# A fused attention and ReGLU kernel whose order of operations comes from a table instead of a greedy planner

## The chip, the cores and the metric

The kernel runs on one core of one Trainium2 chip. The metric is the device time of one execution in microseconds; the median of three runs stands for it. The core has a matrix engine (TensorE, in profiles PE, with its weight loads as PEld), a vector engine (VectorE, DVE), an activation engine (ScalarE, ACT), a general engine (GpSimd, POOL) and an engine that only issues transfers here (SyncE, SP). Each engine runs its own instructions in the order of the program, and waits for the others through semaphores.

## What is computed

Causal attention with a window of 64 positions over 8 batches, 8 heads, 576 positions and 64 dimensions per head, and then a gated layer on all 4608 tokens:

```python
scores = scale * np.matmul(q, k.transpose(0, 1, 3, 2))
mask = (rel >= 0) & (rel < window)                 # window = 64
attn = softmax(np.where(mask, scores, -1e9))
x = np.matmul(attn, v)                             # -> [4608, 512]
gate = np.maximum(x @ w_gate, 0.0)                 # [4608, 1536]
val = x @ w_val
out = (gate * val) @ w_out                         # [4608, 512]
```

Inputs and output are float32; the kernel multiplies in float16 and accumulates in float32.

## The kernel before

**Tiles.** The tokens are cut into nine tiles of 512, numbered 0 to 8. `first_part` (L405 to L510) loads the first q, k, v and weights and computes most of tile 0's attention in an order written out by hand. `second_part` (L512 to L1090) makes the rest.

**Attention of a tile.** A `scores` operation (L385, with the mask added by L377) writes q times k of eight windows and four heads to four PSUM banks; four `exp` on ACT (L645) bring them to SBUF as p. Five `values` operations (L391) multiply by v. DVE takes the reciprocal of the row sums (`recip`, L660), multiplies (`norm`, L398) and transposes to x (`turn`, L403). The next batches' q and k come by `qk_load` on POOL (L347) and are transposed by `qk_turn` on DVE (L353); v comes by `v_load` on POOL (L356), and its shifted rows by `v_copy` (L608, L612, L616) or, from batch 2 on, by `v_move` on SP (L620).

**The gated layer of a tile.** Tile 0 uses plain products: `direct` (L750, a block of gate or value columns), then `relu0` (ACT, L760) and `mul0` (DVE, L762). Tiles 1 to 8 use Strassen-like products P1 to P7 of quarter matrices (L842): the weights' sums are made by `w_form` (L791), those of x by `x_form` (L716). Running sums are taken out of PSUM by `snap` on ACT (L851), completed by `sum` on DVE (L858); the gate half goes through `relu` on ACT (L867) or `last` (L889, straight out of PSUM), and `mult` on POOL (L876) gives the gated g. For one column group the chain between matmuls is short: P1, snap, P6, snap, P7, snap, P4, each product adding to the bank that the snap has just copied.

**The output.** Tiles 0 to 2 use plain `out` products (L916) with `evac` on ACT (L927) and `store` on SP (L931). Tiles 3 to 8 use seven products again (oP1 to oP7, L1005) with sums of g by `g_sum` on DVE (L973), sums of w_out by `wo_form` (L950), snaps (L1016), `osum` on DVE (L1041) and `evac` (L1044).

**What sets the order.** Every operation is an `Op` with a key (the time at which it is wanted, from the constants K), the engines that may run it with an assumed duration for each, the operations that it comes after, and the buffers that it takes and gives back: eight PSUM banks, ten p, twelve float32 `pr` buffers. `Plan.run` (L212 to L255) plays an event-driven schedule while the program is built: whenever an engine is free, `pick` (L178) takes the ready operation with the least key for which buffers are free, with a few rules (a POOL load is held back while the load queue is more than `bl` = 9 us long; a block of small matmuls waits when its instructions would come late). What `run` decides is only the order in which instructions are emitted and which buffer each takes. On the chip nothing of the planner is left: each engine has a fixed line of instructions. `fetch` (L103) is the planner's idea of when TensorE's instructions arrive, 256 at a time; `emit` adds an order between POOL and DVE operations that share a port (L1075 to L1086).

Of the operations, only `w_form`, `wo_form`, a few `x_form` and the `v_copy` may go to one of several engines; the greedy planner takes whichever is free first.

Of the kernel before, what the change touches and what calls it, by code (L numbers as in the profile page):

```python
# [10 lines left out]
FP32 = mybir.dt.float32  # L11
# [9 lines left out]
K = {"T1": 33.417, "STEP": 29.94, "wo1": 24.303, "wo2": 136.509, "q0": 0.81, "q1": 2.61, "q10": -9.561, "q11": 1.093, "v": -0.6, "v1": 1.142, "ql": 1.41, "qt": 0.88, "qti": 4.69, "vl": 0.91, "vc": 0.04, "vm": 1.83, "e": 7.62, "gap": 3.77, "gap1": -1.003, "r": -6.21, "tn": 1.66, "xf": 4.78, "wf": -1.338, "wfj": 2.6, "sn": 2.67, "su": -2.15, "re": 17.5, "mu": -6.61, "la": -4.79, "o0": 11.594, "o0j": 20.432, "o0s": -4.369, "oo": 0.007, "os": 0.386, "oj": 4.81, "gs": -1.18, "fo": 0.015, "fi": 0.098, "fs": 4.74, "fu": 0.27, "W0": 129.92, "TF": 3, "rs": 7.037, "rv": 3.751, "rt": 4.292, "wl": 1.63, "wln": 5.389, "l0": 0.003, "l1": 4.021, "lv": 1.186, "lvs": 12.368, "wo0": 25.921, "db": -7.955, "di": 1.563, "dv": 0.646, "slack": 0.3, "d2": 3.05, "bl": 9.0, "lv0": 18.364, "d": {'0:q0': 0.808, '0:fs': 1.88, '0:la': 1.692, '1:oo': 0.058, '0:fi': 0.024, '1:qt': 3.036, '1:os': -0.226, '0:vc': -1.15, '0:tn': -0.981, '0:qt': 0.904, '0:e': -2.629, '0:sn': 0.475, '0:vm': 0.58, '0:vl': 0.514, '0:ql': 0.128, '0:fu': -2.028, '1:tn': 3.174, '0:re': 0.858, '1:ql': -1.577, '0:xf': -0.14, '0:su': 0.053, '0:gap': 0.391, '0:r': -2.955, '0:oo': -0.042, '0:os': 0.025, '1:vm': 0.483, '1:fo': -0.017, '0:q1': 0.357, '1:sn': 0.632, '0:oj': -0.104, '0:qti': -0.947, '0:gs': -0.096, '0:fo': -0.029, '2:xf': -3.116, '1:oj': -0.851, '1:fu': -1.619, '1:gs': -1.956, '1:vl': 3.671, '1:fs': -1.692, '1:q0': -0.44, '1:re': 17.838, '1:qti': -0.251, '2:vl': -1.63, '1:xf': 0.54, '2:v': 0.897, '2:e': 3.091, '1:vc': -0.626, '2:gap': 1.519, '1:mu': -1.202, '2:oj': 1.272, '2:os': -0.152, '1:gap': -2.068, '1:su': 1.664, '1:q1': 0.09, '1:la': -0.927, '2:fu': -0.861, '2:q0': -1.678, '2:su': -3.121, '1:v': 0.703, '1:r': 0.099, '2:tn': 0.263, '2:mu': -0.767, '2:qti': -1.435, '2:sn': 0.235, '2:qt': 0.357, '3:re': -0.971, '3:su': 1.85, '2:gs': 0.316, '2:vc': -0.222, '2:fi': 0.018, '3:fs': 2.376, '2:oo': -0.024, '3:gs': -0.499, '2:ql': 2.087, '2:re': 1.781, '2:vm': -0.346, '2:la': -0.408, '3:fo': 0.105, '3:qt': -1.251, '3:qti': -0.756, '3:fi': 0.003, '3:r': 4.605, '4:tn': 4.441, '4:fo': 0.176, '3:sn': 1.86, '3:v': -0.191, '3:gap': 0.067, '3:q1': -1.861, '4:v': -2.381, '3:fu': -1.0, '3:e': -2.398, '3:ql': 0.244, '3:q0': -0.417, '4:ql': 1.859, '4:qti': -0.846, '3:oo': 0.017, '3:oj': -1.455, '3:mu': 5.549, '3:vl': -0.094, '3:la': -1.756, '3:os': 0.07, '4:qt': -2.162, '5:v': 2.345, '5:e': -6.12, '5:gap': -0.396, '4:re': 16.126, '4:r': -3.179, '4:os': 0.054, '4:q0': -0.903, '4:gap': -1.023, '4:fu': -1.144, '5:vm': 1.185, '4:fi': -0.029, '4:vm': 1.023, '4:la': 2.23, '4:vl': 0.037, '5:tn': -1.009, '5:r': -1.653, '5:fu': 0.073, '5:re': 3.794, '4:q1': 1.992, '4:sn': 1.164, '4:xf': -1.831, '5:fi': -0.019, '4:mu': 1.169, '4:oj': 1.089, '5:qti': -1.537, '5:fo': -0.021, '5:xf': -1.396, '5:gs': -0.82, '5:mu': -2.334, '5:vc': -0.566, '5:oo': 0.002, '5:q0': -0.047, '4:vc': 0.378, '5:qt': -1.506, '4:fs': 0.072, '5:ql': -0.361, '5:oj': 0.91, '5:fs': -0.532, '5:q1': -0.028, '4:oo': -0.002, '5:la': 0.275, '6:oo': -0.051, '6:vl': -1.345, '6:v': 0.087, '7:vc': 2.102, '6:os': 0.034, '7:fo': -0.026, '6:tn': -1.475, '6:gap': -1.442, '6:xf': 3.27, '6:fi': -0.035, '6:fo': -0.054, '6:fu': -0.179, '6:qt': 0.741, '7:tn': -0.289, '7:vl': -0.177, '6:ql': -0.604, '7:re': 9.431, '7:fi': 0.019, '7:xf': -0.992, '6:vc': -0.932, '7:sn': -0.018, '6:e': 6.905, '6:q1': 1.236, '7:ql': -0.482, '7:e': -4.862, '7:qt': 1.66, '6:mu': -0.73, '7:gap': 0.823, '6:oj': 0.303, '6:q0': 0.231, '6:r': 2.887, '7:su': 1.478, '7:gs': -0.403, '7:q0': -0.079, '7:q1': -0.303, '7:vm': -1.095, '6:gs': -0.02, '7:mu': -0.49, '7:fs': 1.309, '7:la': -0.048, '7:os': 0.117, '7:qti': -1.407, '7:r': -0.97, '7:fu': -0.866, '6:re': 0.021, '6:la': 0.896, '7:oo': -0.007, '6:sn': 0.915}}  # L21
# [5 lines left out]
class Op:  # L27


    def __init__(self, name, key, engines, fn, after, take, give, dma):  # L30
        self.small = 0
        self.count = 0
        self.opens, self.closes = None, False
# [6 lines left out]
        self.end = None  # L40
        self.on = None


class Plan:


    LAG = {"PE": 0.055, "ACT": 0.035, "DVE": 0.035, "POOL": 0.075, "SP": 0.06}
    DRAIN = 0.2
    AHEAD = 20.0
    TURN = 0.093  # L50
    LIMIT = 1e9
    FLIGHT = 8
    STAY = 4.0
# [3 lines left out]
    def __init__(self, free, queue, pools):  # L57
# [4 lines left out]
        self.taken = {}  # L62
        self.open = []
        self.filled = []
        self.known = {e: [] for e in free}
        self.waiting = {e: [] for e in free}
        self.times = []
# [20 lines left out]
    def know(self, o):  # L88
        for e in o.engines:
            self.known[e].append(o)  # L90
            heapq.heappush(self.times, o.ready[e])

    def fetch(self, n, t, dur, keep):
        at, asked, got, come = self.at, self.asked, self.got, list(self.come)
        end = at + n
        while True:
            ask, need = 256 * asked + self.ASK, 256 * got + self.NEED
            nxt = min(ask, need, end)
            t += (nxt - at) * dur / n
            at = nxt  # L100
            if at == end:
                break
            if ask <= need:  # L103
                begin = max([t] + come[-1:])
                begin += max(0.4, min(6.5, self.queue["q"] - begin), min(2.0, self.queue["sp"] - begin))
                come.append(begin + 2.4 + K["slack"])
                asked += 1
            else:
                t = max(t, come[got])
                got += 1  # L110
        if keep:
            self.at, self.asked, self.got, self.come = at, asked, got, come
        return t

    def fill(self, o, t, emit):
        if t - self.free["PE"] < 0.7:
            return
        free = [(self.taken[id(h[n])], h[n]) for pool, h, names in o.take if "bank" in pool for n in names]
        free += [(x[0], x[2]) for pool in ("bank", "bo") for x in self.pools[pool]]
        if free or self.open:  # L120
            since, bank = min(free, key=lambda x: x[0]) if free else (0.0, self.open[-1]["b"])
            since = max(self.free["PE"], since + 0.1)
            n = int((t - 0.25 - since) / 0.165)
            if n > 0:
                self.fetch(2 * n, since, 0.165 * n, True)
                self.filled.append((since, n, t, o.name))
                emit((bank, bool(free)), n)

    def finish(self, o, e, t, dur):
        if e == "PE":  # L130
            if o.opens is not None and o.opens in self.open:
                self.open.remove(o.opens)
            if o.opens is not None and not o.closes:
                self.open.append(o.opens)
            dur += self.TURN * ((o.small > 0) != self.small)
            self.small = o.small > 0
            if o.count:
                dur = self.fetch(2 * o.count, t, dur, True) - t
        end = t + dur
        self.free[e] = end  # L140
        heapq.heappush(self.times, end)
        o.on = e
        if o.dma:
            nbytes, rate, which = o.dma
            self.queue[which] = max(self.queue[which], end + 1.2) + nbytes / rate
            end = self.queue[which] + 0.8
            if e == "POOL":
                self.flight = self.flight[1:] + [end]
                heapq.heappush(self.times, self.flight[0] + 0.1)
# [14 lines left out]
    def grab(self, o, e, t):  # L164
        lag = self.LAG[e]
# [958 lines left out]
```

## Time and profile before

| | |
|---|---|
| median of three runs | 308.23 us (308.16 to 309.68) |
| span of the profiled execution, first to last instruction | 307.2 us |
| the median less that span | 1.0 us |
| TensorE granted clock | 0.999 |
| first matmul / last matmul's start | 1.3 / 303.1 us |
| matmuls | 4772 |
| snaps L851 on ACT | 144, 590 ns each |
| sums L858 on DVE | 144, 678 ns each |
| relus L867 on ACT | 72, 639 ns each |
| mults L876 on POOL | 96, 1283 ns each |
| x_forms L716 on POOL / DVE | 24 of 1160 ns / 8 |

The time of the profiled execution itself is not given apart from its span; the work is compared with the span, and the 1.0 us around it is added to come to the scale of the median. Busy time says how long an engine had an instruction at work. Matmuls are pipelined and the profile models their ends, so TensorE's holes are read from the starts: the distance between two starts, less the usual distance for that shape. An engine's row in a list of groups gives the count, the busy time, the mean duration, and after the bar the idle time just before these instructions with what ended it.

### The profile page before, as it was taken

The numbers are of one execution on the slowest core, as the hardware profiler recorded it, in microseconds if no ns is written. First come the engines' busy times: TensorE is split into PE (matmuls) and PEld (weight loads), VectorE is DVE, ScalarE is ACT, GpSimd is POOL, SyncE is SP. The second block draws the span as 40 slices with busy tenths as digits, with TensorE's granted clock in tenths as the row PEclk, the third lists the DMA queues.
The fourth block names the chain that finished last, engine by engine and source line by source line (L and its number), as shares of the span: only waits on it lengthen the run. The fifth ranks groups of instructions, "written<-read, shape, count | busy, mean of one in ns | idle before, by whom it ended". The sixth has DMA issues, their size and how long they took to land.

```text
span 307.2 us, 11254 instructions
## 1 busy us (share of the span) xinstructions
PE 297.1 (97%) x4772; PEld 240.2 (78%) x4772; DVE 246.2 (80%) x422; ACT 213.0 (69%) x414; POOL 229.8 (75%) x233
## 2 busy tenths in 40 slices
PE   7889999998999999999999999999999999999995
PEld 5475845786757886777888888888888888888884
DVE  5858997988963997887989988878896789595762
ACT  4445335897768787788778786778687886878721
POOL 8696957998999899999189954995479157938520
PEclk9999999999999999999999999999999999999999
DMA  7999999983249953996694194674112011201033
GB/s 219 187 190 206 196 194 198 202 169 22 19 78 150 183 99 75 139 182 136 123 72 82 34 165 120 48 166 37 54 36 69 6 38 37 68 0 36 1 121 120
DMA packets 59074, 32.87 MB, mean 107 GB/s; under 512 B 39440, under 2 KB 53392, under 8 KB 59024
## 3 DMA queue, kind: packets, MB, share of 16 engines
q0 software_dynamic: 46672, 18.29, 51.1%
q1 hardware_dynamic: 12208, 13.80, 14.2%
q8 instruction: 37, 0.61, 0.8%
q14 instruction: 13, 0.11, 0.1%
q10 hardware_dynamic: 144, 0.07, 0.1%
HBM read 37.75 MB, written 9.44 MB: 154 GB/s over the span
## 4 chain that ended last, share of the span: by engine, by line
PE 85%; DMA 8%; POOL 3%; issue 2%; DVE 1%; ACT 0%; ACTq 0%; DVEq 0%; POOLq 0%
PE bank L842 48%; PE bank L1005 18%; PE bank L916 8%; PE bank L391 4%; PE bank L750 3%; DMA wo<-in_moe_w_out_dram 3%; DMA wv<-in_moe_w_val_dram 3%; DMA k<-in_k_dram 2%; PE bank L385 2%; PE bank L377 1%; POOL vs L791 1%; POOL v L356 1%; POOL q L347 0%; POOL k L347 0%; DVE xw L398 0%
## 5 line engine op out<-in xcount | busy, mean ns | idle before, releaser
L876 POOL TENSOR_TENSOR g_sb<-pr,pr 128x512 f16<-128x512 f32 x96 | 121.6, 1283 | 47.7 <-ACT pr L889 16.5
L858 DVE TENSOR_TENSOR pr<-bank,pr 128x512 f32<-128x512 f32 x144 | 92.6, 678 | 24.7 <-PE bank L842 21.9
L851 ACT COPY pr<-bank 128x512 f32<-128x512 f32 x144 | 79.9, 590 | 30.2 <-PE bank L842 27.9
L842 PE MATMUL bank<-xt,vs 128*128 128x256 f16 x384 | 56.7, 273 | 0.0
L842 PE MATMUL bank<-xt,us 128*128 128x256 f16 x384 | 56.2, 273 | 0.0
L867 ACT ACTIVATE pr<-pr 128x512 f32<-128x512 f32 x72 | 45.4, 639 | 5.9 <-DVE pr L858 5.5
L842 PE MATMUL bank<-xt,wg 128*128 128x256 f16 x288 | 42.8, 273 | 0.0
L842 PE MATMUL bank<-xt,wv 128*128 128x256 f16 x288 | 42.7, 273 | 0.0
L842 PEld LDWEIGHTS <-us 128*128 128x128 f16 x384 | 37.0, 98 | 6.5 <-issue 0.2
L842 PEld LDWEIGHTS <-vs 128*128 128x128 f16 x384 | 37.2, 98 | 4.7
L645 ACT ACTIVATE p<-bank 128x512 f16<-128x512 f32 (+1 forms) x68 | 35.7, 592 | 6.7 <-PE bank L385 6.5
L916 PE MATMUL bank<-wo,g_sb 128*128 128x512 f16 x144 | 35.9, 380 | 0.3 <-DMA wo<-in_moe_w_out_dram 0.3
L356 POOL DMA_DIRECT2D v<-in_v_dram x40 | 34.9, 883 | 0.5 <-issue 0.5
L889 ACT ACTIVATE pr<-bank 128x512 f32<-128x512 f32 x48 | 27.1, 601 | 6.7 <-PE bank L842 5.0
L842 PEld LDWEIGHTS <-wg 128*128 128x128 f16 x288 | 27.7, 98 | 4.7
L842 PEld LDWEIGHTS <-wv 128*128 128x128 f16 x288 | 28.1, 98 | 4.2
L1005 PEld LDWEIGHTS <-g_sb 128*128 128x128 f16 x288 | 27.9, 98 | 3.4
L1005 PE MATMUL bank<-wo,g_sb 128*128 128x256 f16 x216 | 28.4, 273 | 0.0
L398 DVE TENSOR_TENSOR xw<-bank,r 128x448 f16<-128x448 f32 (+2 forms) x45 | 25.8, 575 | 1.5
L403 DVE STREAM_TRANSPOSE xt<-xw 128x512 f16<-128x512 f16 (+2 forms) x38 | 25.0, 668 | 0.5 <-ACT xw L506 0.3
L1005 PEld LDWEIGHTS <-ss 128*128 128x128 f16 x216 | 21.0, 98 | 2.5
L916 PEld LDWEIGHTS <-g_sb 128*128 128x128 f16 x144 | 13.5, 98 | 11.3 <-issue 0.3
(95 smaller groups left out, 389.4 us busy)
## 6 DMA issues: line engine op xcount, KB each, us to landing
out_dram<-pr SPq DMA_DIRECT2D x35, 256.0 KB, 2.4
k<-in_k_dram POOLq DMA_DIRECT2D x15, 288.0 KB, 7.5
q<-in_q_dram POOLq DMA_DIRECT2D x15, 288.0 KB, 7.1
v<-in_v_dram POOLq DMA_DIRECT2D x32, 128.0 KB, 6.4
v<-v SPq DMA_DIRECT2D x12, 132.0 KB, 2.6
v<-v SPq DMA_DIRECT2D x24, 66.0 KB, 2.3
wg<-in_moe_w_gate_dram POOLq DMA_DIRECT2D x6, 256.0 KB, 6.6
wv<-in_moe_w_val_dram POOLq DMA_DIRECT2D x6, 256.0 KB, 7.9
```

The costliest lines, as they stand in the source:

```text
L356: nc.gpsimd.dma_start(v16s[b % 2][lo:hi, g, :, 0:64], v[b, :, 64 * g - 64 + lo:64 * g - 64 + hi].rearrange("h p d -> p h d"))
L398: nc.vector.tensor_tensor(x, blocks_of(to, n)[:, :, 0:D].rearrange("p s (c e) -> p s e c", e=2), r[:, :, :, None].to_broadcast([128, n, 2, ...
L403: nc.vector.transpose(xt[:, 2 * hh:2 * hh + 2, c0:c0 + n].rearrange("p e (s c) -> p s e c", c=32), x)
L645: nc.scalar.activation(pp[g][:, 0:n].rearrange("p n c -> p (n c)"), st[g][:, 0:64 * n], ACT.Exp, scale=scale)
L842: nc.tensor.matmul(slot[to][:, HT * m:HT * m + HT], w[:, kk, 128 * m:128 * m + 128], x[:, kk], start=(first and m == 0 and kk == 0), stop= ...
L851: lambda e, hold=hold, slot=slot: nc.scalar.copy(hold["x"], slot["A"]),
L858: nc.vector.tensor_tensor(hold["x"], slot[to], hold["x"], ADD)
L867: lambda e: nc.scalar.activation(hold["x"], hold["x"], ACT.Relu), after=[o])
L876: lambda e: VEC[e].tensor_tensor(gh[:, fs:fs + 2, h], pair(a["x"]), pair(b["x"]), MUL),
L889: lambda e, hold=hold, slot=slot, i=i: nc.scalar.activation(hold["x"], slot["A"], ACT.Copy if i else ACT.Relu),
L916: nc.tensor.matmul(bank["b"][:, 0:c1 - c0], gs[t % 2][:, f, 128 * sub:128 * sub + 128], wo[:, f, c0:c1], start=(j == 0 and i == 0), stop=( ...
L1005: nc.tensor.matmul(bank[to][:, HD * m:HD * m + HD], a[:, f, 128 * m:128 * m + 128], b[:, f], start=(first and m == 0 and f == 0), stop=(f ...
```

## The change

The greedy choice is replaced by a table. `PLACES` holds 1609 numbers, one for each operation in the sequence in which `second_part` makes them; `ON` holds 487 digits, one for each operation that has more than one engine to choose from. `place` writes the place over the key and keeps only the chosen engine; `run` then takes each engine's operations strictly by place. The clock inside the planner still settles which of the engines goes next (and so which buffer is taken) but never the order within one.

```diff
+PLACES = [int(n) for n in """
+11 9 16 18 24 25 43 46 76 78 124 21 20 28 33 67 17 30 6 3 4 51 52 57 54 50 73 70 77 1 5 14 0 19 2 10 7 12 29 44 23 45 8 37 15 49 61 63 89 87
...
+ON = "".join("""
+20201100000010000001101010101001101101100100000102120110000000100000000000000000000000000000000000000001001100010000100111011000000000000000
...
+    def place(self, places, on):
+        choices = [o for o in self.all if len(o.engines) > 1]
+        assert len(places) == len(self.all) and len(on) == len(choices)
+        for o, n in zip(choices, on):
+            e = list(o.engines)[int(n)]
+            o.engines, o.ready = {e: o.engines[e]}, {e: o.ready[e]}
+        for o, key in zip(self.all, places):
+            o.key = key
...
     def run(self, emit):
+        lines = {e: sorted((o for o in self.all if e in o.engines), key=lambda o: (-o.key, -o.n)) for e in self.ENGINES}
+        for _ in self.all:
+            best = None
+            for e in self.ENGINES:
+                if lines[e] and not lines[e][-1].left:
+                    t = self.begin(lines[e][-1], e)
+                    if t is not None and (best is None or t < best[0] - 1e-12):
+                        best = t, e
...
+            t, e = best
+            o = lines[e].pop()
+            self.finish(o, e, t)
+            emit(o, e)
```

More operations get a choice, and small helpers give the instruction for either engine:

```diff
+    def copy_on(e):
+        return nc.scalar.copy if e == "ACT" else VEC[e].tensor_copy
+
+    def relu_on(e, to, x):
+        if e == "ACT":
+            return nc.scalar.activation(to, x, ACT.Relu)
+        else:
+            return VEC[e].tensor_scalar_max(to, x, 0.0)
...
-                forms.append(op("x_form", key + kt("xf") * gap + n, {**pool(512), **(dve16(512) if n == 1 or t == 1 else {})},
+                forms.append(op("x_form", key + kt("xf") * gap + n, any16(512),
...
-                        ran["snap", j, name, i] = op("snap", key - kt("sn"), act(512),
-                                                     lambda e, hold=hold, slot=slot: nc.scalar.copy(hold["x"], slot["A"]),
+                        ran["snap", j, name, i] = op("snap", key - kt("sn"), copies(512),
+                                                     lambda e, hold=hold, slot=slot: copy_on(e)(hold["x"], slot["A"]),
...
-                            ran["relu", j, n, h] = op("relu", key + kt("re"), {"ACT": (0.645, False)},
-                                                      lambda e: nc.scalar.activation(hold["x"], hold["x"], ACT.Relu), after=[o])
+                            ran["relu", j, n, h] = op("relu", key + kt("re"), {"ACT": (0.635, False), "DVE": (0.42, True)},
+                                                      lambda e: relu_on(e, hold["x"], hold["x"]), after=[o])
...
-                        o = op("mult", key + kt("mu"), pool(512),
+                        o = op("mult", key + kt("mu"), {**pool(512), "DVE": (0.68, True)},
```

`relu0`, `last`, the `evac` of the outputs, the output's snaps and `v_copy` get a choice in the same way. Read by the table, these operations run on another engine than before:

| operation | from | to | number |
|---|---|---|---|
| snap (12), last (5), evac (2), relu0 (3) | ACT | DVE | 22 |
| relu | ACT | DVE | 8 (tiles 2, 6, 7, 8) |
| mult | POOL | DVE | 6 (tiles 2, 6, 7 and three in 8) |
| x_form | POOL | DVE | 5, and 2 the other way |
| w_form, wo_form | DVE | POOL | 6, and 1 the other way |
| v_copy | DVE, POOL | ACT, POOL, DVE | 5 |

The rest of the diff changes the planner's own numbers: the times at which engines, banks and p buffers come free at its start, the assumed speed of the load queue, the model of the instruction fetch, a few durations. They reach the chip only through the order of emission and the choice of buffers. A way to load v in float32 and convert it on an engine (`v_raw`, `v_cast`) is added, but its count `VS` is 0, so none is made.

More of the change, by code (lines that the diff above doesn't have):

```diff
@@ L24 @@
+""".split())
 PLANS = []
@@ new lines, in finish @@
+    def finish(self, o, e, t):
+        for pool, holder, names in o.take:
+            for name in names:
+                for p in pool.split("+"):
+                    can = [x for x in self.pools[p] if x[0] + self.LAG[e] <= t + 1e-9]
+                    if can:
+                        item = min(can, key=lambda x: x[:2])
+                        self.pools[p].remove(item)
+                        holder[name] = item[2]
+                        break
+        dur, port = o.engines[e]
+        if port:
+            t = max(t, self.port["POOL" if e == "DVE" else "DVE"])
+            self.port[e] = t + dur
+        begin = t
@@ L664, in value_bank @@
             after = [o for part in parts for o in windows_v(part[2])] + before
-            a = op("values", key, pe(0.031 * m), run, after=after, take=[("bank", to, ("b",))], give=gives)
+            a = op("values", key, pe(0.02 + 0.031 * m), run, after=after, take=[("bank", to, ("b",))], give=gives)
             a.small = a.count = 4 * m
```

279 lines of the change are left out of this document (96 added, 183 removed), and 49 rows, old and new, of the table PLACES.

## The prediction

> **What bounds the kernel now.** I read the shares of busy time first, then busy time by stage, then TensorE's timeline for its holes, and at last the rows of the operations that change engine. The shares (busy us, share of the span, instructions) come first:
>
> ```profile
> PE 297.1 (97%) x4772; PEld 240.2 (78%) x4772; DVE 246.2 (80%) x422; ACT 213.0 (69%) x414; POOL 229.8 (75%) x233
> ```
>
> TensorE works 97% of the span, and the chain of the page gives it 85%. The table cannot take a matmul away, so the gain is limited to TensorE's holes. Busy time by stage (start:end, length, then PE, PEld, DVE, ACT, POOL busy, clock, DMA) shows where holes can be:
>
> ```profile
> 52.00:82.00 30.00, 28.80 (x484) 23.37 (x483) 27.57 (x48) 24.08 (x46) 27.33 (x27) 1.00 0.76 111
> 82.00:112.00 30.00, 30.00 (x472) 21.80 (x471) 21.70 (x36) 23.44 (x44) 28.66 (x29) 1.00 0.91 132
> ...
> 172.00:202.00 30.00, 30.00 (x517) 26.29 (x516) 27.24 (x42) 21.86 (x41) 22.04 (x22) 1.00 0.65 101
> ...
> 232.00:262.00 30.00, 30.00 (x517) 26.18 (x516) 23.64 (x40) 23.10 (x44) 18.23 (x15) 1.00 0.14 46
> 262.00:292.00 30.00, 30.00 (x278) 26.89 (x276) 21.46 (x35) 23.92 (x45) 20.42 (x18) 1.00 0.06 19
> ```
>
> From 82 to 292 us TensorE is full in nearly every stage at a clock of 1.00: nothing is to be won there but turns between kinds of matmul. DVE is the fullest of the others, up to 27.24 and 27.57 of 30 us. The holes lie before 75 us. TensorE's timeline (start, length, what, idle time before it) has them:
>
> ```profile
> 16.64 0.33 PE L750 MATMUL bank<-xt,wv 128*128 128x192 f16 x2
> 17.97 1.33 PE L750 MATMUL bank<-xt,wv 128*128 128x192 f16 x14 [1.01 <-DMA wv<-in_moe_w_val_dram]
> ...
> 28.00 1.47 PE L750 MATMUL bank<-xt,wv 128*128 128x384 f16 x8
> 29.67 1.26 PE L750 MATMUL bank<-xt,wg 128*128 128x128 f16 x16 [0.20 <-DVE xt L403]
> ...
> 41.90 0.21 PE L391 MATMUL bank<-v,p 128*32 128x65 f16 x3
> 42.31 0.39 PE L391 MATMUL bank<-v,p 128*32 128x65 f16 x25 [0.20 <-ACT p L645]
> ...
> 49.30 0.50 PE L391 MATMUL bank<-v,p 128*32 128x65 f16 x28
> 50.13 1.02 PE L916 MATMUL bank<-wo,g_sb 128*128 128x512 f16 x4 [0.33 <-DMA wo<-in_moe_w_out_dram]
> ...
> 70.31 0.21 PE L391 MATMUL bank<-v,p 128*32 128x65 f16 x3
> 71.55 0.82 PE L391 MATMUL bank<-v,p 128*32 128x65 f16 x69 [1.03 <-issue]
> ```
>
> I measure a hole as the distance between two starts less the usual distance for that shape (0.163 us for 384 columns, 0.109 for 256, 0.004 inside a values block), since the modelled ends hide part of it. That gives 1.17 us before wv, 0.37 and 0.20 around the first turned x, 0.40 behind the exps, 0.51 before wo, 1.23 at 71.55, and three more that the timeline shows at 53.2 (0.18, an x_form), 66.5 (0.34, a norm) and 149.1 (0.50, issue).
>
> **The change, part by part.** The operations of second_part are made in the same sequence in both files, so the n-th place and the digits of ON can be put beside the n-th operation. Read so, each engine's line is the old one, shuffled locally: TensorE's 545 operations are displaced by 1 place in the median and 18 at most. The planner's new constants cost nothing on the chip; they act only through the order. VS is 0, so no v_raw or v_cast is made.
>
> *Turns.* The old order enters a block of scores or values 35 times, the new one 32 times. Entering costs 0.093 us (a step of 0.202 from L842 to L391 against 0.109), leaving about 0.1 (0.124 from L391 to L842 against 0.004 to 0.02). Three fewer: 3 x 0.2 = **-0.6**.
>
> *First directs.* The old order runs two gate blocks, then waits for wv until 17.97. The new one puts a gate block of the second half of x between them. Its x is turned at 17.57 (the turn of 0.58 us at 16.99), so TensorE restarts near 17.65 and wv (landed 17.93) is there after 0.65 us. It has not done the two matmuls of 0.08 us that came early before. Worth 0.32 - 0.16 = **-0.16**.
>
> *Values of the rest.* They move from behind 16 of the direct operations to behind 13, and seven (about 0.65 us each) now stand between them and the first block that needs their turned x, against two. The chain is recip 0.16 to 0.18, norm 0.42, the other pair, two turns 0.76: about 2 us under 4.5 us of matmuls. The holes of 0.37 and 0.20 go: **-0.56**. The v copies that feed them move partly to ACT; ACT's row for a copy of 528 columns is 0.63 us against DVE's 0.29 to 0.37, and v has landed by 24.20, so they end near 24.9, ahead of the values at 25.3.
>
> *Exps and wo.* Three operations instead of two stand between tile 1's first scores and values, 2.6 us against 1.73, over four exps of 2.06: the 0.40 goes. The block that waited for wo (landed 50.09) comes behind two more values and one P1, about 0.8 us later, and wo has one qk load less ahead of it in the queue (landings there are 1.4 us apart): the 0.51 goes. Together **-0.91**.
>
> *POOL's line early.* Seven w_forms of 1.16 us now stand together, ahead of the second half of batch 1's q and k. By POOL's rows those loads are issued at about 36.2 instead of 31.90 and 33.61. Loads into an emptied queue took 5.1 to 5.9 us (58.98 to 64.84, 61.93 to 67.00), so the second lands near 43, its turn of 1.25 ends near 44.4, and the scores that need it come at about 44.2. Bounds: 0 (the queue is still full and hides it) to 0.5; I take **+0.2**. What is hidden is the move of four w_forms from DVE to POOL.
>
> *Issue holes.* 2,498 PE records lie before the stall at 71.55 and 5,057 before the one at 149.1: 2,559 apart, ten times 256 within one. They sit at fixed counts of instructions. In the new order the same counts fall in the same values and scores blocks, with the same 4.3 us of matmuls in the stretch before the first. I leave them: **0**, with bounds of -1.7 (both go) and +1.2 (one more as long). The Trainium skill (Runtime: NRT & Kernel Launch, Instruction fetch mechanics) says that instructions are refilled in blocks of 256 and that crossing a boundary is mostly hidden. The spacing agrees; the 1.03 us of idle time does not, and by that rule the 1.7 us would have had another cause that the order might remove.
>
> *Engines.* DVE gains 12 snaps, 5 lasts and 2 evacs (its nearest row is the 128x512 sum from PSUM, 0.678, against 0.59 on ACT; the low bound, scaled from the 128x128 copy of 0.29, is about the same), 8 relus (nearest: the f32 cast of 576 columns, 0.45; taken as 0.42), 3 relu0s and 6 mults (0.68 by the sum; bounds 0.42 and 1.49), and a net 3 x_forms; it loses 4 w_forms and a net wo_form. That is about 20 us more: 266 of 305. The cost on TensorE is nil as long as a stage's DVE work stays under its 30 us, which is what hides it. ACT's 18 us less gains nothing: ACT was late only where TensorE was.
>
> *The tail.* The last tile's third output product now comes six blocks of 0.655 us (3.9) behind the last P3, against nine (5.9). Under it run a sum 0.68, a mult 1.28 behind another one, and two g_sums of 0.42: 4.2 us. **+0.3**.
>
> Sum: -0.6 - 0.16 - 0.56 - 0.91 + 0.2 + 0.3 = -1.73. The profiled execution has a span of 307.2; the median of the runs, 308.23, has 1.0 us more, which I take as the time around the span. So 307.2 - 1.7 + 1.0 = **306.5**.
>
> **Rivals.**
>
> *DVE becomes the bound (slower).* The row that speaks for it is the x_form on DVE (minimum, median, maximum ns):
>
> ```profile
> L716 DVE TENSOR_TENSOR xt<-xt,xt x7: 426/1160/1491, 54.1 to 258.5; 128x512 f16<-128x512 f16 x7
> ```
>
> Alone it takes 0.43, beside POOL's work mostly 1.16: it waits for POOL. Relus, mults and x_forms that read SBUF may do the same, at 0.74 more each (relu 1.16, mult 1.42, x_form 1.16). Tile 2 gains five copies out of PSUM (3.4), three relus (3.5), a mult and an x_form: 9.5. Tile 5 gains three copies and an x_form: 3.2; tile 7 five copies, a relu, a mult and an x_form: 7.1. DVE also sits idle for values (14.5 us over seven tiles, 2.1 a tile). With all of it, DVE needs 21.70 + 9.5 + 2.1 = 33.3 in tile 2's stage (82 to 112), 27.24 + 3.2 + 2.1 = 32.5 in tile 5's (172 to 202) and 23.64 + 7.1 + 2.1 = 32.8 in tile 7's (232 to 262), and 30.1 in tile 8's (three copies, two relus, three mults: 8.6). It decides from 30 us on. With half of the port waits the excess is 1.45 + 2.1 + 1.7 = 5.3: 306.5 + 5.3 = **311.8**. Against it: without port waits (0.42 to 0.68 each) these stages need 29.6, 31.8 and 30.6, the idle time counted in full though queued work fills part of it, and the mults that leave POOL shorten what DVE waits for. The Trainium skill (SBUF — State Buffer, Who interferes with whom) has it as a rule: a DVE instruction with two SBUF inputs and a GpSimd instruction that reads SBUF lock each other out for the whole instruction. The row agrees.
>
> *All holes go.* If the two issue holes and those of 0.18 and 0.34 vanish too (2.25): **304.3**. For it: these blocks run beside loads whose issues move. Against it: the same blocks at the same counts.
>
> *It does nothing.* Both programs are fixed lines per engine, and the new one is a local shuffle; late q and k loads (0.5), a new issue hole (1.2) and thin handoffs may eat the gain. Between TensorE's operations I count eight handoffs in the tiles with under 0.5 us to spare against three: **308.2**.
>
> **How the numbers follow.** The forecast gets 0.50 (305.5 to 307.4), of which 0.33 lies below 306.7; all holes gone 0.12 (303.8 to 305.4); nothing 0.18 (307.4 to 310), of which 0.14 under 309.8; DVE as the bound 0.20 (309.8 to 314). Half a per cent, about what a measurement of this kernel can tell from no change, is 1.54 us: faster 0.45, same 0.31, slower 0.24. The range is 304.3 to 311.8, leaving some 0.04 below and 0.10 above.
>
> **What would show it.** Right: no hole over 0.2 us between 28 and 52 us, TensorE restarting near 17.65, values of tile 1 some 1.5 us earlier, the issue holes still there. Wrong: idle time of PE behind DVE's pr or xw between 82 and 262 us, DVE over 95% in a 30 us stage, or a hole before tile 1's second scores of over 0.5 us.

## The result, and the profile after

The changed kernel takes 323.19 us (median of four runs, 320.9 to 325.43) against 308.52 for the kernel before: a ratio of 1.047, interval 1.041 to 1.053. The forecast was 306.5 in a range of 304.3 to 311.8: the sign, the range and every rival missed it. The profiled execution took 323.8 us, with a span of 322.1 (before: 307.2).

The first look is at the page of the changed kernel: busy time and share of each engine, and the chain that ended last, by engine and by line.

```profile
PE 299.7 (93%) x4772; PEld 240.6 (75%) x4772; DVE 257.3 (80%) x453; ACT 197.9 (61%) x386; POOL 225.1 (70%) x230
PE 71%; DMA 14%; POOL 7%; ACT 3%; issue 2%; DVE 2%; SPq 0%; ACTq 0%; POOLq 0%
```

The same chain in the kernel before:

```profile
PE 85%; DMA 8%; POOL 3%; issue 2%; DVE 1%; ACT 0%; ACTq 0%; DVEq 0%; POOLq 0%
```

TensorE fell from 97% to 93%, and no other engine became full: DVE stands at 80%, as before. TensorE's share of the chain fell from 85% to 71%, and that of DMA rose from 8% to 14%. The page gives 8% of the chain to `out_dram<-pr`, the stores of the output; in the chain of before they do not occur. The idle time of the engines, by what ended it (us in total, times, longest), says who waits for a store:

```profile
ACT pr L869 <- DMA out_dram<-pr: 12.1, 7, 3.0
...
ACT pr L302 <- DMA out_dram<-pr: 5.8, 3, 3.2
...
ACT pr L907 <- DMA out_dram<-pr: 3.3, 2, 2.8
...
DVE pr L304 <- DMA out_dram<-pr: 2.7, 1, 2.7
...
DVE pr L907 <- DMA out_dram<-pr: 1.5, 1, 1.5
...
DVE pr L869 <- DMA out_dram<-pr: 0.8, 1, 0.8
...
DVE pr L1033 <- DMA out_dram<-pr: 0.7, 1, 0.7
```

A snap (now L869, in the output L1033) or a last (L907, or through the helper for relus L302 on ACT and L304 on DVE) waits 26.9 us in all, 16 times, until a store lands. The kernel before has no such wait. Nothing reads an output, so only the buffer can tie them: each of them writes into a `pr` buffer that the store is still reading. TensorE's own waits show that this reaches it:

```profile
PE bank L860 <- ACT pr L869: 6.8, 5, 2.3
PE bank L387 <- ACT pr L907: 1.8, 1, 1.8
...
PE bank L387 <- issue: 1.2, 1, 1.2
...
PE bank L860 <- ACT pr L302: 0.9, 1, 0.9
PE bank L766 <- DMA wg<-in_moe_w_gate_dram: 0.8, 1, 0.8
PE bank L381 <- DVE kT L342: 0.7, 1, 0.7
```

One such hole from near, in the timeline (start, length, engine, what, idle time before it):

```profile
146.38 1.03 SPq L948 DMA_DIRECT2D out_dram<-pr  x2
...
147.33 0.60 PE L860 MATMUL bank<-xt,vs 128*128 128x256 f16 x4
149.18 0.59 ACT L869 COPY pr<-bank 128x512 f32<-128x512 f32 x1 [2.60 <-DMA out_dram<-pr]
...
149.81 0.60 PE L860 MATMUL bank<-xt,wg 128*128 128x256 f16 x4 [1.89 <-ACT pr L869]
```

The store is issued at 146.38 and lands at 149.10. The snap starts 0.08 us later, after 2.60 us of idle ACT, and the P product that adds to the copied bank starts behind it: TensorE has lost 2.05 us. Nine holes of this kind (between 64 and 275 us) make 12.1 us, measured as in the prediction.

| profiled execution, us | span | stalls of PE | turns | last PE start to end |
|---|---|---|---|---|
| before | 307.2 | 10.7 | 9.7 | 4.1 |
| after | 322.1 | 26.1 | 8.9 | 4.8 |

A stall here is a distance between two starts that is over the usual by more than 0.06 us; a turn is such an excess of up to 0.13 us between two lines. The stalls grew by 15.4 us, and 12.1 of them hang on stores. Another 1.7 lie right behind the two holes of 1.1 that end at 65.4 and 66.9: there 16 matmuls of 256 columns follow each other at 0.213 us instead of 0.109, at a granted clock of 0.52 (last section).

### The profile page after: what moved, and what is told of

Same layout as the page of the kernel before. It is cut to its first block, busy times and chain, and to the rows that moved or that the text cites. A ratio compares the mean times of both kernels' runs of the same rounds, so it can differ in the third digit from the quotient of the medians.

```text
span 322.1 us, 11179 instructions
## 1 busy us (share of the span) xinstructions
PE 299.7 (93%) x4772; PEld 240.6 (75%) x4772; DVE 257.3 (80%) x453; ACT 197.9 (61%) x386; POOL 225.1 (70%) x230
## 4 chain that ended last, share of the span: by engine, by line
PE 71%; DMA 14%; POOL 7%; ACT 3%; issue 2%; DVE 2%; SPq 0%; ACTq 0%; POOLq 0%
PE bank L860 41%; PE bank L1022 16%; DMA out_dram<-pr 8%; PE bank L934 7%; PE bank L387 3%; DMA wg<-in_moe_w_gate_dram 2%; PE bank L381 2%; DMA v<-in_v_dram 2%; DMA q<-in_q_dram 2%; POOL us L809 1%; POOL vs L809 1%; ACT pr L869 1%; POOL v L345 1%; PE bank L373 1%; POOL xt L732 1%
## 5 line engine op out<-in xcount | busy, mean ns | idle before, releaser
L894 POOL TENSOR_TENSOR g_sb<-pr,pr 128x512 f16<-128x512 f32 x90 | 113.9, 1279 | 71.8 <-DVE ss L990 16.3
L876 DVE TENSOR_TENSOR pr<-bank,pr 128x512 f32<-128x512 f32 x144 | 94.7, 681 | 20.8 <-PE bank L860 11.3
L869 ACT COPY pr<-bank 128x512 f32<-128x512 f32 x135 | 76.4, 590 | 47.2 <-PE bank L860 32.7
L860 PE MATMUL bank<-xt,vs 128*128 128x256 f16 x384 | 54.9, 273 | 0.0
L302 ACT ACTIVATE pr<-pr 128x512 f32<-128x512 f32 x64 | 39.9, 635 | 4.7 <-DVE pr L876 4.4
L1022 PEld LDWEIGHTS <-g_sb 128*128 128x128 f16 x288 | 28.2, 98 | 3.3
L302 ACT ACTIVATE pr<-bank 128x512 f32<-128x512 f32 (+1 forms) x33 | 18.3, 569 | 18.2 <-PE bank L766 7.0
L394 DVE TENSOR_TENSOR xw<-bank,r 128x448 f16<-128x448 f32 (+2 forms) x45 | 25.0, 569 | 0.7
L342 DVE STREAM_TRANSPOSE kT<-k 128x576 f32<-128x576 f32 x16 | 19.9, 1244 | 3.3 <-DMA k<-in_k_dram 3.1
```

Source lines behind the costliest of these rows:

```text
L302: return nc.scalar.activation(to, x, ACT.Relu)
L342: nc.vector.transpose(dst.rearrange("p (i j) -> p j i", i=32), src)
L394: nc.vector.tensor_tensor(x, blocks_of(to, n)[:, :, 0:D].rearrange("p s (c e) -> p s e c", e=2), r[:, :, :, None].to_broadcast([128, n, 2, ...
L860: nc.tensor.matmul(slot[to][:, HT * m:HT * m + HT], w[:, kk, 128 * m:128 * m + 128], x[:, kk], start=(first and m == 0 and kk == 0), stop= ...
L869: lambda e, hold=hold, slot=slot: copy_on(e)(hold["x"], slot["A"]),
L876: nc.vector.tensor_tensor(hold["x"], slot[to], hold["x"], ADD)
```

## The experiments

**Theory.** In `finish` of before, `end` had become the landing of a transfer by the time its buffers went back to the pool. The changed `finish` keeps the landing in a new name, `done`, and gives the buffer back at `end`, the issue of the store. The planner then hands out a buffer that the chip is still reading. **Rivals:** the new order, and the 55 operations on other engines (DVE's 20 us). In the edits below, "order" stands for the places and "engines" for the digits of ON. "Old" means the order and engines of before, written as a table and run by the changed planner. Each engine's line is then that of before, but the buffers differ, and so do 11 of the waits that `emit` puts between POOL and DVE, since these follow the sequence of emission across the engines. The kernel before took 307.5 to 307.9 us beside these runs.

**Order and engines against the rule of giving back.** One line is changed, and the table or not:

```diff
-            self.pools[self.home[id(holder[name])]].append((end, o.n, holder[name]))
+            self.pools[self.home[id(holder[name])]].append((done, o.n, holder[name]))
```

The new table with the landing:

> The changed kernel with one line of its planner mended: a buffer that a store gives back is free when the store has landed, not when it was issued. Order and engines stay those of the table; only the choice of pr, p and bank buffers differs. Theory A (the 15 us come from snaps, lasts and relus on ACT and DVE that were handed a pr buffer whose store was still in flight): the holes of TensorE that end at a landing of out_dram go (1.1 + 1.1 + 2.0 + 0.6 + 1.4 + 2.0 + 2.4 + 1.4 = 12), so 309 to 312 us. Theory B (the order itself or the operations moved to DVE cost the time): 318 us or more.

The old table with the issue, as in the changed kernel:

> The changed planner with the old order and the old engines as its table, and the rule of the changed kernel: a store's buffer counts as free at its issue. Every engine's line is that of the kernel before; only buffers differ. Theory A: slower than before by 6 to 15 us, with ACT waiting for out_dram (314 to 323). Theory B: 308 to 310, as before.

The old table with the landing:

> The changed planner with the old order and engines, and buffers free at the landing. Every engine's line is that of the kernel before. Both theories: 307.5 to 310, and ACT's waits for out_dram under 3 us; if it is slower, the choice of buffers matters beyond the stores (the planner's starting times or its queue model).

| | given back at the issue | at the landing |
|---|---|---|
| new order and engines | 323.19 | 310.43 (310.17 to 311.07) |
| old order and engines | 310.32 (308.57 to 310.85) | 309.31 (308.35 to 309.77) |

One line is worth 12.8 us in the new order. In the old order it is worth 1.0, which is inside the spread of those runs, and there the theory's expectation failed: a buffer given back too soon costs only if it is taken at once. The time from the issue of a store to the next write into its buffer, over the 29 stores whose buffer is handed out again, shows why: the median is 8.7 us in before and 5.8 with the old table and the issue rule, but 4.05 in the changed kernel, where 27 of 29 are under 6 us. With the landing rule the new table has 5.8. Stores took 2.2 to 5.6 us from issue to landing where ACT waited. Against the 307.5 of the kernel before beside these runs the loss of 15.7 splits into 12.8 for the rule, 1.1 for the new order and engines (310.43 less 309.31) and 1.8 for the old table in the changed planner (309.31 less 307.48).

**More or less rest, and one buffer more.** The changed kernel with a thirteenth `pr` buffer (room for it comes from a shorter tile of zeros) and nothing else:

> The changed kernel as it is (buffers free at the issue), with 13 pr buffers instead of 12; to make room, the zero tile has 256 columns instead of 512 and the one matmul that only keeps TensorE busy reads 256. Theory A: each buffer rests about one taking longer before it is handed out again, so a good part of the waits for out_dram goes: 311 to 318 us, and ACT and DVE wait under 15 us for it against 24. If the buffers are not the cause: 321 to 325.

A smaller dose, with the store's buffer given back 1 us after the issue:

```diff
-            self.pools[self.home[id(holder[name])]].append((end, o.n, holder[name]))
+            self.pools[self.home[id(holder[name])]].append((end + 1.0 if o.dma else end, o.n, holder[name]))
```

> A smaller dose: the new order and engines as in the changed kernel, but a store gives its buffer back 1.0 us after its issue, in the planner's time, where the changed kernel gives it at the issue (323.2) and the mended ones at the modelled landing, 1.9 us, (310.4) or 3 us behind it (310.2). Theory (the rest of the buffer is the cause): between them, 312 to 319, with 4 to 16 us of waits behind out_dram. Rival (the choice of buffers happens to be bad in the changed kernel, whatever the rest): no order in the dose, 310 or over 320.

A larger one, 3 us behind the modelled landing (`done + 3.0 if o.dma else end`), in the new order and in the old; like the smaller dose it touches only what a transfer gives back:

> The new order and engines, with a buffer that a transfer gives back counted as free only 3 us after the planner's own landing time. Theory A, second part (the planner's landing, 1.9 us after the issue, is still early against the measured 2.3 to 5.5): the two holes behind out_dram that were left (1.3 and under 0.7 us) go as well: 308.5 to 309.6 against 310.4. If the rest of the loss lies in the order, it stays at 310 to 311.

> Old order and engines in the changed planner, buffers free 3 us after the planner's landing. Against the same order with buffers free at that landing (309.3) and the kernel before (307.5 to 307.6 on the same chips). If buffers handed out too soon explain the 1.8 us between these two: 307.3 to 308.3. If not (banks and p, or early transfers): 309 to 309.7.

And this larger rest with thirteen buffers, new and old:

> The new order and engines, the give 3 us behind the landing, and a thirteenth pr buffer (the zero tile is 256 columns long). Theory (what is left of the loss is order and engines, not buffers): as with twelve, 309.7 to 310.7, and the holes behind DVE's sums near 60 and 63 us stay, 0.6 and 0.9. Rival (a buffer still comes late somewhere): the holes behind a snap (1.0 near 110 us) go and the time falls to 309.0 or less.

> The control of the run before it: the old order and engines, the give 3 us behind the landing, and thirteen pr buffers. Theory (this order is not short of buffers): 308.9, within 0.5. Rival (twelve buffers cost this order too): under 308.2.

| new order and engines | us | ACT and DVE behind out_dram |
|---|---|---|
| at the issue | 323.19 | 26.9 |
| 1 us after it | 313.17 (311.14 to 314.16) | 11.5 |
| at the modelled landing | 310.43 | 3.2 |
| 3 us behind it | 310.22 (309.74 to 311.45) | 0.4 |
| at the issue, 13 buffers | 311.04 (309.94 to 312.43) | 12.5 |
| 3 us behind it, 13 buffers | 308.59 (307.55 to 311.01) | none |

The time falls with the rest, and falls as well when the planner's rule stays wrong and there is one buffer more. So the cause is the time that a buffer rests, and not a chance assignment. The waits behind stores don't translate one to one: 12.5 us of them cost some 2.5 in the kernel with thirteen buffers (311.04 against 308.59). The last row is 1.6 us under the one with twelve, so the rival of that run was right: a buffer still came late there. What is left in TensorE's own waits of that kernel has no store in it; behind the first matmuls these are the longest, the first for a load, the other for a last, before which ACT's line had waited 1.4 us for a buffer that a mult on POOL was still reading:

```profile
PE bank L935 <- DMA wo<-in_moe_w_out_dram: 1.6, 1, 1.6
...
PE bank L861 <- ACT pr L908: 0.8, 1, 0.8
```

The old order takes 308.93 (308.15 to 309.23) with the larger rest and 309.80 (308.32 to 312.82) with thirteen buffers. So it isn't short of buffers. New less old is +1.3 us with twelve and -1.2 with thirteen, where the two sets of runs overlap: freed of the buffers, neither order is shown to be better.

**Where the order costs.** Old places up to tile 2's second scores and new ones behind them, and the reverse, both with the landing:

> Buffers free at the landing; the old order and engines up to the first scores of tile 2, the new ones from there. Theory A with an early loss: the changed kernel's holes before 52 us (4.6 us in the span, against 2.6 before) come from its early order, so this one is 1.5 to 2.5 us faster than the new order with buffers free at the landing: 307 to 310. If the early order costs nothing, the two are within 0.7 us.

> Buffers free at the landing; the new order up to the first scores of tile 2, the old one from there. It has the new early line and the old tail. If the early line costs (q, k and wo loads issued late): 0.5 to 1.5 over the old order under this rule, 309.8 to 310.8, with a hole before the wo block. If the loss of the new order lies late (tail 0.7 us longer, holes behind out_dram): 309 or less.

They took 310.04 (309.76 to 310.87) and 311.94 (311.37 to 312.76). No half carries the loss; the second has new holes where the halves meet (1.4 each near 68 and 73 us) and one of 1.2 behind wo. This cut told little.

**Engines alone.** The old order with the new engines, and the new order with 33 of the moved operations back on the old engines:

> Old order, buffers free at the landing, but the engines of the new table (30 operations from ACT to DVE, 6 mults and some x_forms from POOL to DVE). Against the old order with the old engines under the same rule (309.3). Rival theory of the prediction (DVE becomes the bound): 312 or more, with PE waiting for DVE. Theory A (the engines are not the loss): 308.5 to 310.5.

> New order with the 3 us rest of the buffers (as in e5, 310.2), and 33 of the operations that the table had moved put back on their old engines (10 could not be, since the planner then runs out of buffers). Theory C (what is left of the loss comes from operations moved to DVE, as the old order with the new engines suggests: 312.6 against 309.3): 308 to 309, and PE no longer waits for DVE pr or ACT pr (1.9 us). If the engines matter only together with the old order: 310 to 311.

The first took 312.62 (311.99 to 313.56), 3.3 us over the old engines in the same order under the same rule: DVE is busy 270 us (87%), and holes of 1.6, 0.5, 0.7 and 0.8 us stand at 66, 84, 93 and 275 us, besides one of 1.4 behind wo. Only those of 0.5 and 0.8 end at an operation on DVE; before the snap that ends the one of 1.6, a last on ACT had waited 2.3 us for a store. The second went the other way than expected: 344.76 (344.05 to 345.99). Its timeline shows the worst place, first ACT, then POOL, then TensorE:

```profile
258.79 0.59 ACT L908 COPY pr<-bank 128x512 f32<-128x512 f32 x1 [3.99 <-DMA out_dram<-pr]
260.25 0.60 ACT L303 ACTIVATE pr<-bank 128x512 f32<-128x512 f32 x1 [0.88 <-DMA out_dram<-pr]
```

```profile
260.92 3.71 POOL L895 TENSOR_TENSOR g_sb<-pr,pr 128x512 f16<-128x512 f32 x3 [8.76 <-ACT pr L303]
```

```profile
PE bank L1023 <- POOL g_sb L895: 7.5, 1, 7.5
```

Each engine keeps to its line, so an operation that has moved into ACT's or POOL's line stands at the place that was made for DVE, and all behind it wait. Here it is a mult, the first of the three in POOL's row. It needs the two lasts in ACT's rows, which had not moved, and they need a buffer; but eight of the twelve `pr` buffers are held for four mults that stand behind it in POOL's line, and the next two to come free are being stored. The loss is in the table itself: the value that the planner's `run` returns is 344.5 us for this kernel and 307.4 without the edit. With all fixes that were then at hand put on top of it the time was 342.78 (341.64 to 343.73), so none of what they mend did it:

> New order with the 3 us rest, the 33 operations back on their engines, POOL's early loads between the w_forms, and the old tail from the last tile of oP7.t7 on. Sum of the parts if each theory holds: 310.2 - 1.5 (engines) - 0.5 (POOL) - 0.7 (tail) = 307.5, as fast as the kernel before. If the order itself loses elsewhere: 309 or more.

**POOL's early line and the tail.** The q, k, v and wo loads put back between the seven w_forms (same engines, places of 15 operations of POOL exchanged), then the old end (order and engines) from the last tile's seventh output product on, both with the larger rest and twelve buffers; then both with thirteen, and the loads alone with thirteen:

> New order as in e5, with one edit: in POOL's early line the q, k, v and wo loads stand between the seven w_forms instead of behind them. My prediction's step on POOL's line: the wo block's wait (0.4 to 1.4 us) goes and q and k land near 40 and 41.5, 309.3 to 310 against 310.2. If the queue hid it: no change (310 to 310.5).

> The new order and engines with the give 3 us behind the landing, and from the last tile's seventh output product on the old order and the old engines. Theory: with the buffers mended the new order is 1.3 us behind the old one under the same rule (310.22 against 308.93), of which 0.73 is the time behind the last matmul's start (4.81 against 4.08 us). So 310.2 - 0.7 = 309.5 (309.0 to 310.0). Rival: the tail is set by the transfers of the last stores and moves nothing: 310.2.

> All that has been found together: the new order and engines, the give 3 us behind the landing, thirteen pr buffers, POOL's early q, k, v and wo loads between the w_forms, and from the last tile's seventh output product on the old order and engines. Theory: 308.6 of the run with thirteen buffers, less the hole behind wo there (1.8 us in its profile, 0 with the loads between) and less 0.7 of the tail: 306.1 to 307.9, no slower than before (307.9). Rival (a hole that is filled early in the span is opened again by the next late transfer, as where the loads alone were moved and the time stayed): 308.2 to 309.5.

> The same with the new tail: the new order and engines, the give 3 us behind the landing, thirteen pr buffers and POOL's early loads between the w_forms. Theory: 0.7 over the run with the old tail, and under the one without the moved loads (308.6): 307.0 to 308.4. Rival: as without the moved loads, 308.4 to 309.8.

With twelve buffers neither moved the time: 311.27 (310.20 to 312.11) and 310.49 (309.07 to 313.18), against 310.22. With thirteen, the loads left it at 308.56 (307.71 to 309.96), against 308.59, though the hole behind wo went from 1.8 us to none: others stand in its place (0.82 us near 41 behind a v copy on DVE, 0.36 at 45 behind a turn). With the old tail as well it is 308.10 (307.50 to 309.25): a ratio of 1.0004 to before, interval 0.998 to 1.003. That is the best of the new order, and it isn't faster than the kernel before.

## Why the prediction was wrong

**The step that failed** is the sentence "The planner's new constants cost nothing on the chip; they act only through the order." They act through the choice of buffers too, as the section on the change says. Two of the changed rules of `finish` decide that choice: when a buffer comes back, and by which clock. The order of the emission was compared operation by operation, the buffers not at all; 12.8 us of the loss lie there, and some part of the 1.8 that the old table costs in the changed planner. No rival named it. The planner cannot see this: its `run` returns 299.2 us for the changed kernel and 302.0 for the same table with the landing rule, so the rule that costs 12.8 us on the chip is a gain of 2.8 in its clock. The other terms are small and mixed. They were forecast to bring 1.73 us; under the landing rule the new order and engines cost 1.1 more than the old ones:

- *Turns*: predicted -0.6, measured -0.8 (9.7 to 8.9, and 8.9 to 9.2 in every kernel of the new order). Right.
- *First directs*: predicted a restart of TensorE near 17.65 and -0.16. It restarted at 17.40, 0.05 us behind the turn of x, which itself came 0.22 earlier, and the hole fell by 0.48 (1.17 to 0.69): as before, two matmuls of the next block came ahead of it, so the 0.16 was not lost. Right in kind. A hole of 0.94 behind wg at 20.36 came in the profile of after alone; none of the new order's other profiles has it.
- *Values of the rest*: the holes of 0.37 and 0.20 before the turned x are gone, as predicted; in their stead 0.35 stands at 25.8 behind an exp, so -0.2 instead of -0.56.
- *Exps and wo*: the 0.40 went. The 0.51 behind wo did not. "wo has one qk load less ahead of it" is true, but the seven w_forms delay its issue too, from 41.17 to 44.55, and it landed at 52.87 instead of 50.09. In after, 1.2 us behind kT and 1.4 of issue stand before it, and only 0.19 is left there; four mended kernels show holes of 0.4, 1.1, 1.4 and 1.8. Against the 0.51 of before that is -0.1 to +1.3 in place of -0.51.
- *POOL's line early*: the loads were issued at 37.4 and 37.9 (predicted 36.2), and kT cost 0.3 and 0.9 near 45 us: +1.2 instead of +0.2, above its bounds of 0 to 0.5. The prediction's own mark of a miss, a hole of over 0.5 before tile 1's second scores, was met. But this too is one execution, in which k was issued 0.9 us later and its turn began 2.1 us later than with the landing rule. The kernels with the landing rule, either rest or thirteen buffers have the same early line, and none of their profiles has a hole of over 0.11 us before these scores: there the term was 0, its lower bound. When the loads were moved back there was no gain, since other holes came in place of the one behind wo: such terms don't add.
- *Issue holes*: predicted to stay at the same counts. They moved: 1,727 and 4,285 PE records lie before those of after (1.44 and 0.56 us), against 2,495 and 5,053 before. The records are counted here as TensorE's and its loads' starts. In both kernels the two are 2,558 apart, ten times 256 less two, and the shift of each is 768, three times 256. The sum, 2.0 against 1.7, lies inside the bounds. With the landing rule, with 3 us more and with thirteen buffers the profiles of the new order have none, so there the term was -1.7 and not 0. The Trainium skill (Runtime: NRT & Kernel Launch, Instruction fetch mechanics) gives blocks of 256, which agrees with both distances; which of the many boundaries costs something is not in its rule, and no run here settles it.
- *Engines*: DVE grew by 11 us, not 20, and its new rows are as priced or a little over (next fences). In after only one hole of over 0.3, of 0.34, ends at an operation that had moved to DVE, a last that itself waited for a store; with 3 us of rest 0.60 and 0.94 stand behind sums on DVE near 60 and 63 us, with thirteen buffers too 0.51. DVE is busy 27.3 of 30 us at most in the stages of the first two. In the old order the port waits that the rival feared are there: its x_forms took up to 1.56 us, its relus 2.20, its mults 1.73, all beside POOL's work. But DVE's fullest stage has 27.9 of 30 us, and only 1.3 us of the holes end at DVE. So the rival had the price of an operation right for that order; that DVE became the bound is not shown, there or in the new one.
- *Tail*: +0.7 instead of +0.3, and by another way. The g_sum chain opened no hole. Five stores of 256 KB are issued between 314.8 and 317.0, and the last two small ones behind them took 2.56 and 2.47 us to land; in before they took 1.84 and 1.70 behind two large ones. So the end is 4.82 us behind the last PE start against 4.09. In the times of the runs the old tail is worth 0.5 (308.56 to 308.10), which is inside their spread.

The x_form on DVE, whose 1160 ns before carried the rival, in the changed kernel (minimum, median, maximum ns):

```profile
L732 DVE TENSOR_TENSOR xt<-xt,xt x6: 406/425/553, 55.6 to 243.4; 128x512 f16<-128x512 f16 x6
L732 DVE TENSOR_TENSOR xt<-xt x5: 404/419/582, 56.9 to 244.9; 128x512 f16<-128x512 f16 x5
```

```profile
L304 DVE TENSOR_SCALAR pr<-pr x8: 408/420/625, 95.3 to 302.6; 128x512 f32<-128x512 f32 x8
```

```profile
L894 DVE TENSOR_TENSOR g_sb<-pr,pr x6: 681/693/1034, 102.1 to 304.7; 128x512 f16<-128x512 f32 x6
```

The waits for POOL are all but gone: 425 instead of 1160 ns for the x_form, 420 for a relu, 693 for a mult. The Trainium skill's rule of the lock (SBUF — State Buffer, Who interferes with whom) was no bound here: at their new places these operations overlap with a computing instruction of POOL by 0.5 us at most, where six of the seven x_forms of the prediction's row did by 0.66 to 1.21.

One term of the base was small too: the time around the span was taken as 1.0 us. In the later runs of the kernel before it is 1.9 to 2.0, in the new order's 1.7. So the profiled execution of before, with its span of 307.2, was some 0.9 us longer than the median run (an estimate from 307.2, 1.9 and 308.23), and a hole that was read in it need not be in every execution.

**What stays open.** The old order and engines, run by the changed planner with every rest that was tried, take 308.9 to 309.8 us, 1.1 to 1.9 more than before, though each engine's line is the same. The buffers, the form of 24 copies and 11 of the waits between POOL and DVE differ. One of these waits can be seen (lines in the last section): in before, a w_form on POOL waits 1.19 us for DVE and starts behind the v copies near 26 us; in the old order under the landing rule it starts during the first of them, which takes 2.15 us instead of 0.45. Holes of 0.85 and 0.82 us follow at 28 and 31 us, where before has 0.36 and 0.20. So the sequence across engines reaches the chip as well, and a comparison of each engine's line doesn't see it. No run isolates it from the buffers.

## What to carry to other kernels

A schedule that is written out as a table is the order, the engines and the buffers, and whoever compares two must put all three side by side, and the waits that the sequence of emission adds between engines; "they act only through the order" has to be read off the code that hands out buffers, not assumed. A transfer that reads a buffer holds it until it has landed, and a planner that gives it back at the issue puts the next writer, if it takes the buffer at once, and all that stands behind it on that engine, behind the transfer. To find such a cause, replay the old table in the new machinery and the new table with the old rule: the four kernels of the first table told the 13 us apart from the rest, while cutting the order in halves told little, and moving engines by themselves brought losses of their own, because a fixed line fits only the engines that it was made for.

## What the runs showed of the hardware

- In 15 of the 16 waits of the changed kernel the next write into a stored buffer starts 0.08 to 0.12 us after the store has landed (0.02 in the other). From issue to landing a 256 KB store took 2.2 to 5.6 us where it was waited for, with a median of 2.8 in after and 2.4 in before.
- The same two copies of v took 2.47 us on DVE in the old order under the landing rule and 0.77 in before. The first of the two took 2.15 against 0.45. The second line of each pair is POOL's w_form, which lies inside that copy in the one kernel and behind both copies in the other:

```profile
26.05 2.47 DVE L625 COPY v<-v 64x528 f16<-64x528 f16 x2
...
26.86 1.17 POOL L810 TENSOR_TENSOR us<-wg 128x512 f16<-128x512 f16 x1
```

```profile
25.56 0.77 DVE L608 COPY v<-v 64x528 f16<-64x528 f16 x2
...
27.09 1.15 POOL L791 TENSOR_TENSOR us<-wg 128x512 f16<-128x512 f16 x1 [1.19 <-DVE us L791]
```

  That the w_form is what slowed the copy is likely, but no run isolates it.
- The granted clock of TensorE is 0.94 in the stage from 52 to 82 us of the changed kernel, where before has 1.00. All of that lies in one stretch of 3.4 us, right behind the two holes of 1.1 us, and not behind the longer ones of 2.0 to 2.4 us at 78, 150 and 177 us, where the clock stays at 1.00 (the PEclk column, after the busy times of PE, PEld, DVE, ACT and POOL):

```profile
52.00:82.00 30.00, 26.11 (x478) 19.84 (x462) 22.66 (x42) 18.41 (x35) 22.80 (x24) 0.94 0.87 127
```

```profile
64.00:67.00 3.00, 1.12 (x10) 0.71 (x8) 0.80 (x2) 2.24 (x5) 0.94 (x2) 1.00 0.52 159
67.00:70.50 3.50, 3.50 (x18) 2.55 (x18) 2.08 (x3) 2.32 (x5) 3.49 (x4) 0.52 0.14 10
70.50:74.00 3.50, 3.35 (x145) 2.80 (x143) 2.50 (x6) 2.89 (x6) 3.50 (x6) 0.99 0.70 101
```

  In the 3 us ahead of it TensorE was busy 1.12 us. What sets the clock down is not shown.
- TensorE's holes behind which the profile finds nothing but issue (with over 0.15 us of idle, from 20 us on) are twelve in the 20 profiles of this case, at most two in one, and eleven profiles have none. Each lies at a count of PE records (starts of TensorE and of its loads) that leaves a remainder of 187 to 191 when it is divided by 256. Most such counts show no hole.
